# First MLP layer: the second product of the last two token blocks by seven block products, sums of weights on VectorE, a fourth raw buffer

## The chip, the cores and the metric
One core of a Trainium2 chip runs the whole program. TensorE (PE) multiplies, VectorE (DVE) and GpSimd (POOL) work element by element, ScalarE (ACT) does functions and copies, SyncE (SP) issues most transfers (DMA), POOL the accumulating ones. The metric is the device time of one execution, in microseconds (us); three runs of the kernel before are shown.

## The reference
Chunked attention over 3072 tokens, then two MLP layers in float32:

```
x = attention(q, k, v, mem_k, mem_v)        # 3072 x 512, windows of 32 queries
h = x @ w_in;   g = softplus(h)             # 512 -> 2048
y = g @ w_out                               # 2048 -> 512: the product that is changed
h2 = y @ w_in2; g2 = prelu(h2, alpha)       # second layer
out = g2 @ w_out2
```

## The kernel before
Tokens go in six blocks of 512 (`NB`). A float32 operand is a high and a low part, and a product takes three matmuls (high high, high low, low high). All matmuls of the MLPs have 128 x 128 weights against 512 columns.

**First layer.** There are 96 steps (`steps`), one for a block and 128 of the 2048 hidden features (`f`, 16 for each block). A step has `pe_h` (12 matmuls into `ps_hh`, one of two banks), softplus on ACT (`act_first`, tile `ta`), the high part on ACT (`high`, tile `g`), the low part on DVE (`low`), and `pe_out` (12 matmuls that add to four banks `ps_o`, one for each quarter of the 512 outputs). The two banks for `ps_hh` mean that step i+2 can't start before the softplus of step i has read its bank. `drain_one` and `drain_to` bring a finished block to `y_dram`. Attention of later blocks (24 tiles of 128 tokens: scores `s`, maximum `m`, shift `c`, `exp` on ACT, sum `n`, share `w`, transposes `t`, copy `pt`, values `v*`, split into `x`) lies between the steps. Softplus and exp need different tables on ACT, so an exp stands between two loads of a table.

**Weights.** `load_raw` brings float64 words into a pool of three rooms (`raw`), DVE turns them into float32 (`ab` to `cv`), ACT and DVE or POOL split them (`high_w`, `low_w`). Weights of the second layer are brought in during the first; `weight_sums` makes four sums of each set of blocks on POOL (tile `wsum`), `split_task` splits blocks and sums, and all go to DRAM (`in_ops`, `out_ops`).

**Second layer.** Blocks go in pairs. `quad` makes the first product and `second` the second product, each by seven block products in place of eight (`PASSES`: S1, A11, S4, S2, S3, A12, A22), 8 items for each pass, 6 matmuls for each item, into `ps_q`. In `second`, `load_w_out` brings 1 MB for every four items, POOL's accumulating DMAs (`SUMS`) and `prepare` (loads and sums of `y` for the next pair, tiles `yraw`, `yt`, `xop`) lie beside it. The last step's `pe_out` runs within the first `quad` (`between`).

**Order.** Up to about 90 us it is written by hand (`OPENING`). Behind that `schedule` gives every piece an engine, a length, a due time (with offsets in `O`), what it comes after, and rooms that it takes and gives; `Plan.run` lists them, and engines then take their instructions in that order, each in its own queue. SP and POOL queues too are in order: an issue that waits holds all behind it.

Of the kernel before, what the change touches and what calls it, by code (L numbers as in the profile page):

```python
# [57 lines left out]
HK = 2 * P  # L58

# [28 lines left out]
RUNS = 8  # L88
O = {'km': -55.97, 's': 11.7, 'm': 28.21, 'c': 66.61, 'e': 31.62, 'n': 45.26, 'r': -92.5, 'w': 94.58, 't': 85.64, 'pt': 82.79, 'v': -20.27, 'xh': 136.06, 'xl': -8.55, 'first': 47.53, 'gap': -183.71, 'second': 20.97, 'gap2': -27.69, 'raw': 41.75, 'ab': -85.86, 'cl': -61.09, 'ca': 10.82, 'cb': 74.39, 'cc': -95.76, 'wh': -29.12, 'wl': -22.45, 'odd': 97.94, 'sp': 116.5, 'hi': 37.44, 'lo': 2.59, 'out': 17.61, 'wait': 0.05, 'sloads': -125.79, 'km0': 68.55, 'km1': 28.97, 's0': -25.87, 's1': 2.3, 'm0': -192.19, 'm1': -112.61, 'c0': -31.95, 'c1': -25.21, 'e0': -51.53, 'e1': -16.47, 'n0': -131.79, 'n1': 72.42, 'r0': -17.47, 'r1': -5.18, 'w0': 52.91, 'w1': -43.08, 't0': -1.99, 't1': 39.24, 'pt0': -100.96, 'pt1': 70.29, 'v0': 21.52, 'v1': 14.34, 'xh0': -72.64, 'xh1': 5.24, 'xl0': 133.53, 'xl1': -30.69, 'by0': -46.78, 'by1': 30.48, 'va': -0.63, 'vb': 176.94, 'vc': -46.03, 'vd': 155.73, 'ra': -58.02, 'rb': 154.89, 'rc': 130.18, 'wld': 105.54, 'dra': -108.27, 'ca0': 58.14, 'ca1': -5.43}
# [33 lines left out]
class Plan:  # L123
# [16 lines left out]
    PORT = {"ab", "ab2", "cl", "cl2", "ca", "cb", "cv", "cv2", "n", "r", "w", "lo", "wl", "km", "sums2", "sl2", "wd", "ysum", "yd", "y4"}  # L140
# [87 lines left out]
def attention_mlp_mlp_kernel(ctx: ExitStack, tc, qk, v, w1, w2, consts, out):  # L228
# [11 lines left out]
    rpool = ctx.enter_context(room_pool("raw", 3))  # L240
# [12 lines left out]
    y_dram = dpool.tile([DM, NTOK], F32, name="y_dram")  # L253
    in_ops = dpool.tile([NQ, P, 2, 7, HK], F32, name="in_ops")
# [55 lines left out]
    def high_w(k):  # L310
        if k % 2 == 0:
            W[k // 2] = wpool.tile([P, 2, 2 * DM], F32R, tag="w", name="wsplit")
        act.copy(out=W[k // 2][:, 0, k % 2 * DM:(k % 2 + 1) * DM], in_=words[0, k])

    def low_w(k, eng):
        w = W[k // 2][:, :, k % 2 * DM:(k % 2 + 1) * DM]
        eng.tensor_tensor(out=w[:, 1, :], in0=words.pop((0, k)), in1=w[:, 0, :].bitcast(F32), op=ALU.subtract)
# [20 lines left out]
    def weight_sums(q, second):  # L338
# [291 lines left out]
    def drain(ps_of, b):  # L630
        for m, ps in enumerate(ps_of):
            if m % 2 == 0:
                room = rpool.tile([P, 2, DM], F32, tag="raw", name="o_sb")
            drain_one(m, ps, room[:, m % 2, :])
            drain_to(m, room[:, m % 2, :], b, False)

# [16 lines left out]
    def pe_out(i):  # L653
        b, f, first, final = steps[i]
        if first:
            acc[b] = acc_banks()
        out_sums(acc[b], g_sp.pop(i), W[f][:, :, DM:], first, final)
        if final and i == len(steps) - 1:
            drain(acc.pop(b), b)
# [5 lines left out]


# [7 lines left out]
    def raw_y(name):  # L674
        return late["x"].tile([P, N2], F32, tag="yraw", name=name, bufs=6)
# [8 lines left out]
    def sum_y(p, h, n):  # L684
        if n == 0:
            y_raw[p, h, T2] = raw_y("yt")
            y_raw[p, h, T3] = raw_y("yt")
# [278 lines left out]
    def prepare(p):  # L966
# [4 lines left out]
        for h in range(2):  # L971
            load, add, last, split = ((1, 8, 12, (11, 13, 15, 17, 19, 21, 23)), (19, 26, 30, (29, 31, 38, 44, 45, 47, 48)))[h]
# [26 lines left out]
    def schedule(when):  # L999

        plan = Plan({"h": 2, "ta": 2, "g": 1, "pa": 2, "s": 1, "tb": 1, "tb2": 1, "pair": 1, "tb0": 1, "tb1": 1, "word": 3, "raw": 3, "qk": 1, "v": 1,
                     "acc": 4, "y": 6, "w": NF, "x": 2})
# [10 lines left out]
        for n, k in enumerate(order):  # L1013
# [8 lines left out]
            add(("wh", k), "ACT", 0.62, need - O["wh"], lambda k=k: high_w(k), [("cv", n)] + ([("ds", 15)] if k == 26 else []) + ([("wh", k - 1)] if k % 2 else []), [] if k % 2 else ["w"])  # L1022
# [4 lines left out]
        for i, (b, f, first, final) in enumerate(steps):  # L1027
            t = when[i]
            x = [("xl", TB * b + c) for c in range(TB)]
            add(("h", i), "PE", 2.72, t, lambda i=i: pe_h(i), [("wl", 2 * f)] + (x if f == 0 else []) + ([("h", i - 1)] if i else []), ["h"])  # L1030
# [3 lines left out]
            if i == last:  # L1034
                break
            add(("out", i), "PE", 2.72, t + O["out"], lambda i=i: pe_out(i), [("lo", i), ("wl", 2 * f + 1)] + ([("out", i - 1)] if i else []),
                ["acc"] * 4 if first else [], ["g"] + (["w"] if i > last - NF else []))
            if final:
                room = ["w"] if f < HALF else ["x"]
                def begin(i=i, f=f):  # L1040
                    staged[i] = ((wpool if f < HALF else xpool).tile([P, 4, DM], F32, tag="w" if f < HALF else "x", name="o_sb"))
                add(("db", i), "", 0.0, t + 12, begin, [("out", i)], room if f < HALF else [])
# [6 lines left out]
                add(("ds", i), "", 0.0, 0, nothing, [("dd", i, m) for m in range(4)], [], room if f < HALF else [])  # L1049
# [7 lines left out]
        def tile(t, prev, due, step=None):  # L1057
# [22 lines left out]
            after_s += ([("t", TB - 1)] if t == TB else []) + ([("pt", prev)] if t > 2 * TB else []) + ([("h", step)] if step else [])  # L1080
            after_s += [("xl", TB + c) for c in range(TB)] if t == 2 * TB else []
            joint = t > 3 * TB
# [11 lines left out]
            else:  # L1094
                add(("c", t), "DVE", 0.6, due - when_due("c"), lambda: a_shift(t), [("m", t)], [], [] if start or joint else [sb])
# [35 lines left out]
        for j in range(4 * NQ):  # L1131
            q, e = divmod(j, 4)
            k, due = halves[j], when[24 + 64 * j // (4 * NQ)]
            dma(("raw2", j), 0.4, 1.9, due - 8, lambda j=j: load_raw(1, halves[j]), [("cv2", j - 1)] if j else [("raw", 2 * NF - 1)], ["raw"])
# [4 lines left out]
            def split_task(name, src, n, to, after, us, give):  # L1139
# [9 lines left out]
                add(("sl2",) + name, "POOL", us, due + 5, low_piece, [("sh2",) + name], [], give)  # L1149
                dma(("ss2",) + name, 0.45 * len(to), n / DM * 1.9, due + 6, store_piece, [("sl2",) + name], [], ["raw"])  # L1150

            if e % 2:
                z, k0 = e // 2, 4 * q + e // 2
                add(("sums2", q, z), "POOL", 3.2, due + 3, lambda q=q, z=z: weight_sums(q, z),
                    [("cv2", j)] + ([("sl2", q - (not z), 1 - z, 4)] if j > 1 else []), ["raw"])
# [3 lines left out]
                split_task((q, z, 0), lambda k=wide: words[1, k], DM, operands_at(q, z, A12 if z else A11, 2), [("sums2", q, z)], 1.4, ["word"])  # L1159
                split_task((q, z, 1), lambda k=narrow, part=part: words[1, k][:, part], HK, operands_at(q, z, A11 if z else A22, 1), [("sl2", q, z, 0)], 0.9, ["word"])  # L1160
                for n in (0, 2):
                    split_task((q, z, 2 + n), lambda q=q, z=z, n=n: sums[q, z][:, n:n + 2, :], DM, operands_at(q, z, S1 + n, 2),
                               [("sl2", q, z, 1 + n)], 1.4, ["raw"] if n else [])
                    if n == 0:
                        add(("sl2", q, z, 3), "", 0, 0, lambda: None, [("sl2", q, z, 2)])

        add("switch", "", 0, 0, switch_pools, [("xl", t) for t in range(NT)])
        for h in range(2):
            due = when[last - 8 + 4 * h]
            dma(("yl", h), 1.6, 3.2, due, lambda h=h: load_y(0, h), ["switch"], ["y"] * 4)  # L1170
            add(("ysum", h), "DVE", 2.1, due + 8, lambda h=h: [sum_y(0, h, n) for n in range(3)], [("yl", h)], ["y"] * 2)
# [96 lines left out]
```

## Time and profile before
| | us |
|---|---|
| runs shown (median) | 1085.9, 1088.45, 1087.64 (1087.64) |
| the profiled execution, its own time | 1090.2 |
| span of its instructions | 1088.1 |
| PE busy | 1066.2 (98%) |
| DVE, ACT, POOL busy | 704.4, 543.1, 171.8 |

The span is counted from the first to the last instruction; 2.1 us of the execution lie around it. "Busy" of an engine is the time in which one of its instructions was under way. The profile names the helper's line for all instructions, so tiles tell them apart: `ps_hh` and `ps_o` are the first layer's products, `ps_q` the second layer's, `ps_a` attention.

### The profile page before, as it was taken

How to read it: one execution, taken by the hardware profiler on the slowest of the kernel's cores; microseconds unless marked ns; L12 is line 12 of the kernel's file. 1: busy time of each engine (PE TensorE's matmuls, PEld its weight loads, DVE VectorE, ACT ScalarE, POOL GpSimd, SP SyncE). 2: the span in 40 equal slices, each digit the busy share in tenths (PEclk: the TensorE clock that was granted, in tenths of full speed). 3: DMA queues.
4: the chain of work that ended last, by engine and by line, in shares of the span. 5: the costliest groups of instructions: out<-in, count | busy, mean ns of one | idle time of the engine just before them, and what ended most of it. 6: DMA issues, size and time to landing. Idle time of an engine off the chain costs nothing.

```text
span 1088.1 us, 18751 instructions
## 1 busy us (share of the span) xinstructions
PE 1066.2 (98%) x7281; PEld 871.0 (80%) x7281; DVE 704.4 (65%) x1182; ACT 543.1 (50%) x940; POOL 171.8 (16%) x213
## 2 busy tenths in 40 slices
PE   6799999999999999999999999999999999999998
PEld 4568888778888888888888888888888888888886
DVE  5789988655554564345455156678666779566976
ACT  4564435455453454444344255664555755456643
POOL 0010112434234233222323100000000010000000
PEclk9989999999999999999999999999999999999999
DMA  8885674767656564535355173799875999856904
GB/s 203 209 188 182 188 196 126 187 184 192 197 165 183 175 170 128 187 120 166 111 180 191 61 288 126 282 282 322 200 280 174 327 298 256 259 203 256 372 0 78
DMA packets 156441, 214.69 MB, mean 197 GB/s; under 512 B 78656, under 2 KB 108480, under 8 KB 149440
## 3 DMA queue, kind: packets, MB, share of 16 engines
q1 hardware_dynamic: 152048, 196.58, 56.9%
q0 software_dynamic: 4032, 16.78, 8.1%
q8 instruction: 57, 0.93, 0.4%
q14 instruction: 32, 0.26, 0.1%
q10 hardware_dynamic: 272, 0.13, 0.0%
HBM read 154.74 MB, written 46.14 MB: 185 GB/s over the span
## 4 chain that ended last, share of the span: by engine, by line
PE 92%; DMA 5%; SPq 2%; DVE 1%; issue 0%; DVEq 0%
PE ps_q L76 42%; PE ps_hh L76 23%; PE ps_o L76 23%; PE ps_a L76 3%; DMA raw<-in_w_dram 3%; SPq L76 2%; DMA v<-in_v_dram 1%; DVE word L76 1%; DMA qk<-in_qk_dram 0%; DVE x L76 0%; DVE g L76 0%; DVE sm L76 0%; DVE wsplit L76 0%; DVE v L76 0%; DVE c L76 0%
## 5 line engine op out<-in xcount | busy, mean ns | idle before, releaser
L76 PE MATMUL ps_hh<-x,wsplit 128*128 128x512 f32 x1152 | 282.5, 394 | 1.9 <-DVE x L76 1.1
L76 PE MATMUL ps_o<-g,wsplit 128*128 128x512 f32 x1152 | 280.4, 392 | 0.8 <-DVE g L76 0.8
L76 PEld LDWEIGHTS ps_hh<-x,wsplit 128*128 128x128 f32 x1152 | 216.7, 189 | 49.0 <-DVE x L76 1.6
L76 PEld LDWEIGHTS ps_o<-g,wsplit 128*128 128x128 f32 x1152 | 214.3, 188 | 46.0 <-DVE g L76 1.1
L76 PE MATMUL ps_q<-xop,win 128*128 128x512 f32 x1008 | 229.1, 389 | 0.0
L76 PE MATMUL ps_q<-g,wout 128*128 128x512 f32 x1008 | 229.1, 389 | 0.0
L76 PEld LDWEIGHTS ps_q<-g,wout 128*128 128x128 f32 x1008 | 189.0, 188 | 39.5
L76 PEld LDWEIGHTS ps_q<-xop,win 128*128 128x128 f32 x1008 | 189.2, 188 | 39.3
L76 DVE TENSOR_TENSOR g<-ta,g 128x512 fp32r<-128x512 f32 x96 | 70.9, 738 | 132.5 <-ACT g L76 132.2
L76 ACT CAST g<-gb 128x512 fp32r<-128x512 f32 x168 | 100.8, 622 | 89.8 <-PE ps_q L76 66.1
L76 DVE TENSOR_TENSOR g<-gb,g 128x512 fp32r<-128x512 f32 x168 | 114.2, 686 | 35.2 <-ACT g L76 33.2
L76 ACT CAST g<-ta 128x512 fp32r<-128x512 f32 x96 | 59.6, 621 | 120.8 <-PE ps_o L76 120.6
L76 ACT ACTIVATE ta<-ps_hh 128x512 f32<-128x512 f32 x96 | 57.5, 599 | 119.8 <-PE ps_hh L76 116.5
L76 DVE SCALAR_TENSOR_TENSOR word<-raw,word 128x512 int32<-128x512 int32 x128 | 91.5, 715 | 2.7
L76 ACT ACTIVATE tp<-gb 128x512 f32<-128x512 f32 x48 | 30.4, 633 | 91.4 <-DVE gb L76 91.4
L76 POOL TENSOR_TENSOR wst<-wsum,wst 128x512 fp32r<-128x512 f32 x32 | 45.0, 1406 | 127.0 <-ACT wst L76 121.3
L76 DVE SCALAR_TENSOR_TENSOR gb<-gb,tp 128x512 f32<-128x512 f32 x48 | 33.2, 692 | 44.0 <-ACT tp L76 44.0
L76 DVE TENSOR_SCALAR word<-word 128x512 f32<-128x512 f32 (+1 forms) x128 | 57.3, 452 | 2.1
L76 POOL TENSOR_TENSOR wst<-word,wst 128x512 fp32r<-128x512 f32 (+1 forms) x32 | 34.2, 1068 | 140.3 <-ACT wst L76 135.1
L76 DVE TENSOR_SCALAR word<-raw 128x512 int32<-128x512 int32 x64 | 30.0, 471 | 39.8 <-DMA raw<-in_w_dram 26.9
L76 ACT ACT_TABLE_LOAD x38 | 48.8, 1283 | 11.1 <-DVE nm L76 10.5
L76 POOL DMA_DIRECT2D gb<-gb x12 | 10.4, 864 | 277.3 <-DVE g L76 168.4
(87 smaller groups left out, 860.6 us busy)
## 6 DMA issues: line engine op xcount, KB each, us to landing
wout<-out_ops SPq DMA_DIRECT2D x42, 1024.0 KB
raw<-in_w_dram SPq DMA_DIRECT2D x64, 512.0 KB
win<-in_ops SPq DMA_DIRECT2D x24, 1024.0 KB
win<-in_ops SPq DMA_DIRECT2D x24, 768.0 KB
out_ops<-wst SPq DMA_DIRECT2D x56, 256.0 KB
in_ops<-wst SPq DMA_DIRECT2D x24, 512.0 KB
gb<-gb POOLq DMA_DIRECT2D x12, 1024.0 KB, 13.7
qk<-in_qk_dram SPq DMA_DIRECT2D x24, 320.0 KB
```

What stands on the lines that cost most here:

```text
L76: i = getattr(self.engine, name)(*args, **kw)
```

## The change
For blocks 4 and 5 (`LP` = 4) steps have `pe_h` and softplus only. `g_first` and `g_kept` keep the results in eight 1 MB tiles (`gb`), the even features negated or with their differences. Behind them stand 56 items of six matmuls (`last_out`) into banks named `ps_q`, by the same seven passes as in `second`, with `g_high` on ACT and `g_low` on DVE ahead of each; four DMAs and eight additions on POOL make their sums (`BYDMA`, `("gs", ...)`). Their weights come from a new DRAM tile `outs_1`: the plain blocks stored as they are split (`("ac", ...)`), the sums made anew from the two parts on DVE (`whole_again`, `sums_of_first`, `low_part`), split, stored, and loaded by `load_last`. The loads of `y` for the second layer's first pair, `prepare`'s work of that pair and the first `win` lie beside these items.

W is laid out by two steps and by product (`weight`), so that rooms of w_out come free while w_in is used. The second layer's sums move from POOL to DVE for the first 8 of 16 sets (`BYPOOL`), and their low and high parts are made 1024 wide at once. `raw` has 4 rooms in place of 3, `yraw` 4 in place of 6; the tile `s` of late attention is now `pt`. The offsets `O` are other numbers, and a plan is chosen by the end of all pieces (`whole`).

```diff
-    rpool = ctx.enter_context(room_pool("raw", 3))
+    rpool = ctx.enter_context(room_pool("raw", 4))
...
+    def whole_again(q):
+        t = sums[q] = parts_room(q == 0)
+        w = W[q, 1].bitcast(F32)
+        dve.tensor_tensor(out=t[0].bitcast(F32).rearrange("p a k -> p (a k)"), in0=w[:, 0, :], in1=w[:, 1, :], op=ALU.add)
+
+    def sums_of_first(q):
+        t = sums[q]
+        a11, a21, a12, a22 = (t[0].bitcast(F32)[:, k, :] for k in range(4))
+        four_sums(dve, t[1], a11, a12, a21, a22)
...
+    def g_kept(i):
+        b, f, _, _ = steps[i]
+        a = g_a.pop(i)
+        if b == LP:
+            dve.tensor_scalar(out=slot(f % 2 * 2, f // 2), in0=a, scalar1=-1.0, scalar2=None, op0=ALU.mult)
+        else:
+            dve.scalar_tensor_tensor(out=slot(1, f // 2), in0=G[0, f // 2], scalar=-1.0, in1=a, op0=ALU.mult, op1=ALU.subtract)
...
+    def last_out(n):
+        i, q = divmod(n, NQ)
+        ka = PASSES[i][0]
+        more = ka == A12
+        if q == 0:
+            last_ps[ka] = last_ps[A11] if more else [bank({A11: "h", S4: "pa"}.get(ka, "acc")) for _ in range(2)]
+        g, w = g2.pop(n), w_out[-1, n // 4][:, n % 4]
+        for m in range(2):
+            for k, (a, e) in enumerate(((0, 0), (0, 1), (1, 0))):
+                pe.matmul(
+                    last_ps[ka][m], lhsT=w[:, a, m * P:(m + 1) * P], rhs=g[:, e, :], start=not more and q == 0 and k == 0,
+                    stop=q == NQ - 1 and k == 2, skip_group_check=more,
+                )
...
+            add(("gh", n), "ACT", 0.62, due - O["gh"], lambda n=n: g_high(n), after + ([("gh", n - 1)] if n else []), g)
+            add(("gl", n), "DVE", 0.72, due - O["gl"], lambda n=n: g_low(n), [("gh", n)])
...
-    pairs(lambda: pe_out(last))
+    pairs(lambda: None)
```

PE's order around block 4's steps. Before, `ps_hh` (first product) and `ps_o` (second) alternate, attention (`ps_a`) between them:

```order
L76 MATMUL ps_hh<-x,wsplit 128x512 x12
L76 MATMUL ps_a<-cst,s_sb 128x128 x4
L76 MATMUL ps_o<-g,wsplit 128x512 x12
L76 MATMUL ps_hh<-x,wsplit 128x512 x12
L76 MATMUL ps_a<-pt,v 64x32 x32
L76 MATMUL ps_a<-qk 32x64 x32
L76 MATMUL ps_o<-g,wsplit 128x512 x12
```

Now, from the middle of block 4 to the second layer (`ps_q<-g,wout` ahead of the first `ps_q<-xop,win` are the new items):

```order
L80 MATMUL ps_hh<-x,wsplit 128x512 x48
L80 MATMUL ps_a<-cst,pt 128x128 x4
L80 MATMUL ps_hh<-x,wsplit 128x512 x12
L80 MATMUL ps_a<-pt,v 64x32 x32
L80 MATMUL ps_hh<-x,wsplit 128x512 x180
L80 MATMUL ps_q<-g,wout 128x512 x6
L80 MATMUL ps_hh<-x,wsplit 128x512 x12
L80 MATMUL ps_q<-g,wout 128x512 x6
L80 MATMUL ps_hh<-x,wsplit 128x512 x12
L80 MATMUL ps_q<-g,wout 128x512 x6
L80 MATMUL ps_hh<-x,wsplit 128x512 x12
L80 MATMUL ps_q<-g,wout 128x512 x318
```

The second products of blocks 4 and 5 have left the places between the first products and stand behind them, 318 of their 336 matmuls in one stretch. ACT's order at an exp within block 4's steps, before (`ta` is softplus, `s_sb` the exp, `g` and `wst` high parts):

```order
L76 ACTIVATE ta<-ps_hh 128x512
L76 CAST wst<-word 128x256
L76 ACT_TABLE_LOAD
L76 ACTIVATE s_sb<-s_sb 128x512
L76 CAST g<-ta 128x512
L76 ACT_TABLE_LOAD
L76 ACTIVATE ta<-ps_hh 128x512
```

And now, with the queue's waits:

```order
L80 ACTIVATE ta<-ps_hh 128x512 [waits PE_49,Activation_49]
L80 ACT_TABLE_LOAD
L80 ACTIVATE pt<-pt 128x512 [waits DVE_49]
L80 ACT_TABLE_LOAD [waits PE_49]
L80 ACTIVATE ta<-ps_hh 128x512 [waits Activation_49]
L80 CAST wst<-wst 128x1024 [waits DMAHW2_49,DMAHW1_49,Pool_49]
L80 ACTIVATE ta<-ps_hh 128x512 [waits DVE_49,PE_49,Activation_49]
```

The cast of `g` is gone, a 1024 wide cast that waits for POOL and transfers stands ahead of a softplus. DVE's order late in the new items (`yt<-yraw` is the first sum of the second half of `y`):

```order
L80 TENSOR_TENSOR g<-gb,g 128x512 x2
L80 TENSOR_TENSOR yt<-yraw 128x512
L80 TENSOR_TENSOR yt<-yraw,yt 128x512
L80 TENSOR_TENSOR yraw<-yraw 128x512
L80 TENSOR_TENSOR g<-gb,g 128x512 x3
```

The sums stand ahead of the low parts of items 45 to 47 here. Before, sums of `y` for the first pair stood among first-layer steps, like this:

```order
L76 TENSOR_TENSOR g<-ta,g 128x512
L76 TENSOR_TENSOR yt<-yraw 128x512
L76 TENSOR_TENSOR yt<-yraw,yt 128x512
L76 TENSOR_TENSOR yraw<-yraw 128x512
L76 TENSOR_TENSOR g<-ta,g 128x512
```

What moved is the cover: there a low part was wanted every two products, here for every item of six matmuls.

## Rows read from the trace of the kernel before

**Rows 1.** Page, part 1: busy us (share of span) and instructions.
```profile
PE 1066.2 (98%) x7281; PEld 871.0 (80%) x7281; DVE 704.4 (65%) x1182; ACT 543.1 (50%) x940; POOL 171.8 (16%) x213
```

**Rows 2.** PE's waits, whole span: us in total, times, longest.
```profile
PE ps_s L76 <- POOL qk L76: 6.8, 5, 2.7
PE ps_x L76 <- DMA v<-in_v_dram: 2.3, 3, 1.6
...
PE ps_hh L76 <- DVE x L76: 1.1, 1, 1.1
```

**Rows 3.** Stretches: length, busy (instructions) of PE, PEld, DVE, ACT, POOL; PEclk, DMA, GB/s.
```profile
40.00:60.00 20.00, 16.00 (x255) 12.12 (x256) 15.42 (x35) 11.53 (x18) 3.99 (x9) 0.91 0.89 197
...
520.00:540.00 20.00, 20.00 (x90) 16.57 (x89) 6.19 (x11) 6.18 (x11) 7.18 (x7) 1.00 0.30 102
...
700.00:720.00 20.00, 20.00 (x90) 16.48 (x89) 15.65 (x25) 13.83 (x25) 2.62 (x3) 1.00 1.04 336
720.00:740.00 20.00, 20.00 (x90) 16.56 (x89) 12.72 (x20) 12.00 (x22) 1.72 (x2) 1.00 1.02 293
740.00:760.00 20.00, 20.00 (x90) 16.54 (x89) 19.41 (x33) 10.40 (x18) 0.86 (x1) 1.00 1.03 320
760.00:780.00 20.00, 20.00 (x90) 16.57 (x89) 15.29 (x24) 10.27 (x18) 0.00 (x0) 1.00 0.83 185
```

**Rows 4.** Chain that ended last, in order of time: start, us, what.
```profile
614.80 2.72 PE ps_hh L76 x12
617.52 5.44 PE ps_o L76 x24
...
631.12 451.62 PE ps_q L76 x1992
```

**Rows 5.** SP's waits, 44 to 47 us.
```profile
SPq L76 <- DVE g L76: 1.6, 1, 1.6
```

**Rows 6.** Order of time, PE, 40 to 80 us: start, us, instruction, [idle before].
```profile
53.02 1.58 PE L76 MATMUL ps_s<-qk 64*32 64x64 f32 x64 [2.71 <-POOL qk L76]
...
77.15 7.12 PE L76 MATMUL ps_hh<-x,wsplit 128*128 128x512 f32 x23 [1.10 <-DVE x L76]
```

**Rows 7.** Order of time, ACT at an exp, 492 to 498 us.
```profile
494.06 1.28 ACT L76 ACT_TABLE_LOAD   x1
495.36 0.63 ACT L76 ACTIVATE s_sb<-s_sb 128x512 f32<-128x512 f32 x1
496.00 1.28 ACT L76 ACT_TABLE_LOAD   x1
497.30 0.60 ACT L76 ACTIVATE ta<-ps_hh 128x512 f32<-128x512 f32 x1
```

**Rows 8.** ACT's waits for rooms that a store holds, whole span.
```profile
ACT wst L76 <- DMA out_ops<-wst: 10.8, 12, 2.6
```

**Rows 9.** Costliest groups: count, busy us, mean ns, idle before.
```profile
L76 DVE TENSOR_TENSOR g<-gb,g 128x512 fp32r<-128x512 f32 x168 | 114.2, 686 | 35.2 <-ACT g L76 33.2
L76 ACT CAST g<-gb 128x512 fp32r<-128x512 f32 x168 | 100.8, 622 | 89.8 <-PE ps_q L76 66.1
```

**Rows 10.** SP's issue and DVE's use of the second half of `y`.
```profile
721.58 7.12 SPq L76 DMA_DIRECT2D yraw<-y_dram  x4
...
739.54 0.69 DVE L76 TENSOR_TENSOR yt<-yraw 128x512 f32<-128x512 f32 x1 [1.66 <-DMA yraw<-y_dram]
```

**Rows 11.** DMA issues: count, KB each, us to landing.
```profile
wout<-out_ops SPq DMA_DIRECT2D x42, 1024.0 KB
...
win<-in_ops SPq DMA_DIRECT2D x24, 1024.0 KB
win<-in_ops SPq DMA_DIRECT2D x24, 768.0 KB
...
gb<-gb POOLq DMA_DIRECT2D x12, 1024.0 KB, 13.7
```

More of the change, by code (lines that the diff above doesn't have):

```diff
@@ L656, in pe_out, with slot, g_first @@
             acc[b] = acc_banks()
-        out_sums(acc[b], g_sp.pop(i), W[f][:, :, DM:], first, final)
-        if final and i == len(steps) - 1:
-            drain(acc.pop(b), b)
+        out_sums(acc[b], g_sp.pop(i), weight(f, 1), first, final)
+    def slot(k, q):
+        if q % 4 == 0:
+            slots[k, q // 4] = wpool.tile([P, 4, N2], F32, tag="w", name="gb")
+        G[k, q] = slots[k, q // 4][:, q % 4, :]
+        return G[k, q]
+    def g_first(i):
+        b, f, _, _ = steps[i]
+        to = slot(3, f // 2) if b > LP and f % 2 else tpool.tile([P, N2], F32, tag="ta", name="ta", bufs=2)
+        act.activation(out=to, in_=h_ps.pop(i), func=AF.Softplus)
+        g_a[i] = to
@@ new lines, in load_last, with keep, came_of @@
+    def load_last(j):
+        t = w_out[-1, j] = wpool.tile([P, NQ // 2, 2, HK], F32R, tag="w", name="wout")
+        sp.dma_start(out=t.bitcast(F32), in_=outs_1[PASSES[j // 2][0], j % 2])
+    def keep(key, m, tag):
+        kept_1[key, m] = tpool.tile([P, N2], F32, tag=tag, name="u2", bufs={"tb": 1, "tl": 1, "word": 3}.get(tag, 2))
+        return kept_1[key, m]
+    def came_of(d, b, m):
+        if m == 0:
+            c_1[d, b] = rpool.tile([P, 2, N2], F32, tag="raw", name="c")
+        return c_1[d, b][:, m, :]
@@ L685, in sum_y @@
         if n == 0:
-            y_raw[p, h, T2] = raw_y("yt")
-            y_raw[p, h, T3] = raw_y("yt")
+            two = rpool.tile([P, 2, N2], F32, tag="raw", name="yt")
+            y_raw[p, h, T2], y_raw[p, h, T3] = (two[:, e] for e in range(2))
         to, a, b = ((T3, T1, B11), (T2, B22, T3), (T1, B22, T1))[n]
@@ L1048, in schedule @@
                         [("dr", i, m)], eng="POOL" if adds else "SP")
-                add(("ds", i), "", 0.0, 0, nothing, [("dd", i, m) for m in range(4)], [], room if f < HALF else [])
+                add(("ds", i), "", 0.0, 0, nothing, [("dd", i, m) for m in range(4)], [], room if over else [])
         add("corners", "DVE", 2.4, 0, no_corners)
@@ L1167, in schedule @@
-        add("switch", "", 0, 0, switch_pools, [("xl", t) for t in range(NT)])
+                split_task((q, z, 0), lambda k=wide: words[1, k], DM, operands_at(q, z, A12 if z else A11, 2), [("cv2", j if z else j - 1)], 1.4, ["word"])
+                split_task((q, z, 1), lambda k=narrow, part=part: words[1, k][:, part], HK, operands_at(q, z, A11 if z else A22, 1), [("cv2", j - 1 if z else j)], 0.9, ["word"])
+                for k in range(2):
+                    add(("wd2", q, z, k), "", 0, 0, nothing, [("sums2", q, z), ("sl2", q, z, k)], [], ["word"])
@@ new lines, in schedule @@
+        for q in range(NQ):
+            due = when[44 + 2 * q] - O["so"]
+            rooms = ["w"] if q else ["raw"] * 2
+            add(("rc", q), "DVE", 1.4, due - O["sq"], lambda q=q: whole_again(q), [("wl", 4 * q + 1), ("wl", 4 * q + 3), ("raw", 2 * NF - 1)] + ([("sl1", q - 1)] if q else []), rooms)
+            add(("sums1", q), "DVE", 1.65, due - O["sr"], lambda q=q: sums_of_first(q), [("rc", q)])
+            add(("sh1", q), "ACT", 1.05, due + 1, lambda q=q: high_part(sums[q]), [("sums1", q)])
+            add(("sl1", q), "DVE", 1.4, due + 1 - O["sc"], lambda q=q: low_part(dve, sums[q]), [("sh1", q)])
+            dma(("ss1", q), 0.9, 3.8, due + 2, lambda q=q: store_parts(sums.pop(q), sums_at(outs_1, q, 1)), [("sl1", q)], [], rooms)
+            dma(("ac", q, 0), 0.9, 1.9, when[24 + 3 * q] - O["ac"], lambda q=q: store_to(DM, W[q, 1][:, :, DM:], first_at(q, A12, 2)), [("wl", 4 * q + 1), ("wl", 4 * q + 3), ("raw", 2 * NF - 1)] + ([("i", "ac", q - 1, 1)] if q else []))
+            dma(("ac", q, 1), 0.45, 0.95, when[24 + 3 * q] - O["ac"], lambda q=q: store_to(HK, W[q, 1][:, :, :HK], first_at(q, A11, 1)), [("i", "ac", q, 0)])
+            add(("wf", q), "", 0, 0, nothing, [("out", LH - NF + 2 * q + 1), ("rc", q), ("ac", q, 0), ("ac", q, 1)], [], ["w"])
@@ L1168, in schedule @@
+        for k, n, m in ((3, 23, [("gs", 1, 3, q) for q in range(NQ)]), (0, 39, []), (2, 47, [("gs", 1, 2, q) for q in range(NQ)]), (1, 55, [])):
+            add(("sf", k), "", 0, 0, nothing, [("gl", n)] + m, [], ["w"] * 2)
         for h in range(2):
-            due = when[last - 8 + 4 * h]
-            dma(("yl", h), 1.6, 3.2, due, lambda h=h: load_y(0, h), ["switch"], ["y"] * 4)
-            add(("ysum", h), "DVE", 2.1, due + 8, lambda h=h: [sum_y(0, h, n) for n in range(3)], [("yl", h)], ["y"] * 2)
+            due = end + 10 + 26 * h
+            dma(("yl", h), 1.6, 2.9, due, lambda h=h: load_y(0, h), ["switch", ("out", last + 7)], ["y"] * 4)
+            add(("ysum", h), "DVE", 2.1, due + 8, lambda h=h: [sum_y(0, h, n) for n in range(3)], [("yl", h)], ["raw"])
@@ L1191, in attention_mlp_mlp_kernel, with whole @@
         when = came + [came[-1] + 2.72 * 2]
-    plan = min(plans, key=lambda x: x.done["out", last - 1])
+    def whole(x):
+        d = x.done
+        return max(d["out", last + 7 * NQ], d["win0",], d["win1",] - 8, d["yd", 1, T4] - 6, d["cc", 1, 0, 1] - 3, max(d.values()) - 6)
+    plan = min(plans, key=whole)
     for name, (since, until) in plan.idle.items():
```

214 lines of the change are left out of this document (155 added, 59 removed).

## The prediction
> **What bounds the kernel now.** The first view is the page's list of busy times: PE is under way in 1066.2 of 1088.1 us [rows 1], so 21.9 us are all that waits and ends leave to gain, and anything larger must come from fewer matmuls. The second is PE's waits over the whole span: its waits are for `qk` from POOL (6.8 us in five), for `v` from DMA (2.3) and once for `x` from DVE (1.1) [rows 2], all of them before 78 us in the order of time; the last two are in [rows 6]. The third is a table of stretches: from 520 us on every 20 us have 20.00 us of PE at a granted clock of 1.00 [rows 3]. The fourth is the chain that ended last, which gives the price of a matmul where PE never stops: 12 of the first product take 2.72 us, 24 of the second 5.44, and 1992 of the second layer 451.62 [rows 4], each time 0.2267 us. So behind the opening the time is the number of 128 x 512 matmuls times 0.2267 us, and every other engine counts only where it can't keep up with that.
>
> **Removed.** Blocks 4 and 5 have 2 x 16 steps of 12 matmuls in the second product, 384. Now there are 56 items of 6, 336. The first products, attention and the second layer keep their counts. 48 x 0.2267 = **10.9 us less**, all on PE's path.
>
> **The opening.** The order of PE, ACT and POOL up to about 80 us stays as it is. What changes is the fourth room of `raw`: SP's queue stands 1.6 us for a room that DVE has to free [rows 5], and behind that load in the same queue are loads of `qk` and `v`. These end, through POOL's copy of `qk`, at PE's idle 2.71 us ahead of `ps_s` at 53.02 and later at its 1.10 us for `x` at 77.15 [rows 6]. Best case: both go, −3.8. Worst: nothing goes, since DMA engines are at 0.89 of their time in 40 to 60 us [rows 3] and an earlier load only pushes others; a fourth load in flight might even delay a `qk` by up to 1 us, +1. I take SP's own wait, **−1.6**, the only part of it that the room removes by itself.
>
> **The steps without a second product.** Before, 5.44 us lay between two first products' starts; now, from step 64, they follow each other at 2.72 us on two banks, save for attention's matmuls. PE can go from step i+1 to i+2 without a stop if softplus i ends within 2.72 us of step i's end. Softplus is 0.60 us [rows 7], which leaves 2.12. An exp with its two table loads is 1.28 + 0.63 + 1.28 = 3.19 us [rows 7]. If it starts right behind softplus i−1, that is 0.60 us into a step of 2.72, softplus i starts 1.07 late and ends 1.67 after its step, and nothing stops. If it starts just when the step ends, softplus ends at 3.79, 1.07 over. The order leaves four tiles of attention that can meet this: 0 to 4.3 us. ACT's casts of `wst` that wait for stores are the other part: 12 waits of 10.8 us together, 0.9 on average, the longest 2.6 [rows 8]. The mean fits into 2.12, the longest passes it by 0.5; three such would make 1.5. So 0 to +6; I take one late exp, **+1.0**, since the exps hang on `m` and `c` from DVE, at 6.19 of 20 us in such a stretch [rows 3] and so rarely late.
>
> The Trainium skill speaks against this part: "ScalarE: Activation LUTs", section "What ACT_TABLE_LOAD costs", adds a drain of about 1380 ns to the load's 1283 ns, some 2.66 us for a switch. The trace bears out the load and not the drain: the softplus begins 1.30 us after the load began [rows 7]. By the page every switch back would take 2.66 + 0.60 = 3.26 us (an estimate from that page), 0.54 over the step, some 2 us in four tiles, and the forecast below would be 1079.5 in place of 1077.4.
>
> **The 56 items.** An item is 6 x 0.2267 = 1.36 us on PE; ahead of it are a cast on ACT of 0.622 and a subtraction on DVE of 0.686 us [rows 9]. Items 4 to 7 have two rooms `g` only, so a cast waits for the end of the item two before it: 1.31 us of work in 1.36, with hand-overs between. That is 0 to 0.2 us for each of about five items, up to +1; **+0.3**. Later items take rooms of `raw` too and run like the second layer's, on the same cast and subtraction, where PE doesn't stop.
>
> The second half of `y` needs rooms that DVE frees in the first half's sums. In the new order SP's last `yraw` load can be issued only about six items, 8.2 us, ahead of the low part of item 45, and DVE's sums stand ahead of that low part: a late load holds items up. Before, 10.8 us lay between the end of SP's issue (721.58 + 7.12 = 728.70) and the first sum at 739.54, and DVE waited 1.66 of it for the load [rows 10], while DMA engines were full (1.02 and 1.03) [rows 3]. By that row the load is up to 2.6 us late; with rooms in hand, items 42 to 44 hide one to two of these. 0 to +3; **+1.0**.
>
> **Costed at nothing.** DVE gets eight sets of w_out: a sum 1024 wide, four sums 256 wide and a low part 1024 wide. At 0.686 us for 512 columns [rows 9] that is about 1.4 + 1.4 + 1.4 = 4.2 us a set, 34 us; eight sets of sums from POOL are 1.4 each, 11 us. It uses 6.19 of 20 us in the stretch where they stand [rows 3], so in 200 us there would be some 138 free for these 45. Should that cover be gone, the low parts of steps are late; in 740 to 760 us, though, DVE was at 19.41 of 20 and PE still had its 20 [rows 3]. Stores to `outs_1` go out in the same stretch at DMA share 0.30 [rows 3]. The first item's weights are issued some four steps, 11 us, ahead of it, like the 1 MB of an accumulating DMA that lands in 13.7 us with its additions [rows 11]; if they are late, 1 to 3 us come on top, which I leave in the range.
>
> **The sum.** −10.9 − 1.6 + 1.0 + 0.3 + 1.0 = −10.2. The profiled execution took 1090.2 us, so 1080.0 in its like. The median of the shown runs, 1087.64, is 2.6 lower: **1077.4 us**.
>
> **Rivals.**
> *ACT sets the pace in steps 64 to 95.* All four exps fall late, or casts that wait stand ahead of softplus: +4.3 to +6 in place of +1.0, so 1080.7 to 1082.4 us. For it: in the new order a 1024-wide cast with waits for POOL and two transfers stands directly ahead of a softplus. Against it: ACT has about 0.60 of 2.72 us taken by softplus in these steps, as the cast of `g` has gone. Chance 0.15.
>
> *DMA sets the pace in the items: slower than before.* Their weights are 14 x 1.05 MB = 14.7 MB, the four accumulating DMAs 4.2, `y` 2.1 in and 2.1 out, and two pairs of `win` 2 x (1.05 + 0.79) = 3.7 (sizes: [rows 11]); 26.8 MB in the items' 76 us and some 20 us ahead of them, 280 GB/s. In 700 to 780 us the chip moved 336, 293, 320 and 185 GB/s, 283 on average, with DMA engines full in the first three [rows 3]. So it fits, with little over. At 280 nothing is lost. At 248 GB/s the transfers need 108 us, 12 more: the gain is used up. At 240 they need 111.7 us, and the time is 1077.4 + 15.7 = 1093 us. For it: accumulating transfers read as much as they write. Against it: 320 and 336 were held beside like work, and the demand for weights alone is 1.05 MB in 5.44 us, as in the second layer before. It decides from about 245 GB/s down. Chance 0.07.
>
> *The change doesn't deliver.* If all 56 items were bound by their rooms at 0.1 to 0.2 us each, 5.6 to 11.2 us would go back: 1083 to 1088.6. Against it: only eight items are confined to two rooms. Chance 0.05, mostly within 0.2%.
>
> *The opening gives both waits.* −3.8 in place of −1.6: 1075.2, and 1073 to 1074 if the items and the exps cost nothing too. Chance 0.11.
>
> **How the numbers follow.** Forecast 0.62, ACT 0.15, DMA 0.07, no delivery 0.05, opening 0.11. The range is from 1072.9, all costs at nothing and both opening waits gone (1090.2 − 10.9 − 3.8 − 2.6), to 1083, ACT's upper end: **1073 to 1083**, which leaves out the last two unfavourable cases. A measurement of this kernel tells about 0.2%, 2.2 us, from no change. Faster by more: 0.62 + 0.15 + 0.11 + 0.01 = 0.89; within it 0.04; slower 0.07.
>
> **What would show it.** In the profile after: 336 more matmuls into `ps_q` and 384 fewer into `ps_o`; 0.2267 us a matmul on the chain from the last first product to the end. PE's waits should have the opening's entries, smaller than 2.71 and 1.10, and the start of the uninterrupted PE some 1.6 us ahead of 77.15. A wait of `ps_hh` for `ta` over 4 us in total means ACT's rival; a wait of `ps_q` for `wout` by DMA, with DMA share at 1 over the whole of the items, means the DMA rival; many short waits of `ps_q` for `g` on DVE mean rooms; one wait for `g` behind `yt` means the late `yraw`. The forecast is wrong if PE's idle behind 80 us is over 8 us, or if the opening is longer than before: then the load order, and not the matmul count, decides.

## The result: slower, since a load of y in the second layer comes late

| | before | after |
|---|---|---|
| median of the runs, us | 1086.88 (4 runs) | 1095.64 (4 runs: 1093.45, 1095.38, 1095.89, 1096.64) |
| the profiled execution, its own time | 1090.2 | 1093.45 |
| span of its instructions | 1088.1 | 1091.7 |

The ratio to before is 1.0076 (interval 1.0056 to 1.0097): 0.8% slower, where the prediction had 1077.4 us and 0.89 on faster. The profiled execution is the fastest of the four, 2.2 us below their median.

The page's first part and PE's waits over the whole span (us in total, times, longest) answer to [rows 1, 2]:

```profile
PE 1058.8 (97%) x7229; PEld 861.2 (79%) x7233; DVE 793.2 (73%) x1318; ACT 561.3 (51%) x958; POOL 161.8 (15%) x177
```

```profile
PE ps_q L80 <- DVE g L80: 8.7, 5, 6.5
PE ps_s L80 <- POOL qk L80: 4.9, 2, 2.7
PE ps_a L80 <- issue: 2.1, 1, 2.1
PE ps_o L80 <- issue: 1.6, 1, 1.6
PE ps_hh L80 <- DVE x L80: 1.5, 2, 1.1
```

PE is 7.4 us less busy (48 matmuls fewer at 0.2267 us would be 10.9; part of the difference is the clock, below), and yet the span is 3.6 us longer. The first line of the waits is new: `ps_q` is the second layer and the new items, where PE never waited before. PE's order of time (start, us, instruction, [idle before]) has the places and the borders of the stages:

```profile
73.84 5.55 PE L80 MATMUL ps_hh<-x,wsplit 128*128 128x512 f32 x23 [1.11 <-DVE x L80]
...
616.20 4.01 PE L80 MATMUL ps_q<-xop,win 128*128 128x512 f32 x17
...
692.36 2.90 PE L80 MATMUL ps_q<-g,wout 128*128 128x512 f32 x12
...
745.91 19.33 PE L80 MATMUL ps_q<-g,wout 128*128 128x512 f32 x74 [6.54 <-DVE g L80]
...
778.00 2.20 PE L80 MATMUL ps_q<-xop,win 128*128 128x512 f32 x9
...
854.15 2.21 PE L80 MATMUL ps_q<-g,wout 128*128 128x512 f32 x9
...
902.17 5.26 PE L80 MATMUL ps_q<-g,wout 128*128 128x512 f32 x18 [1.38 <-DVE g L80]
...
933.71 2.65 PE L80 MATMUL ps_q<-xop,win 128*128 128x512 f32 x11
```

The first layer with its new items ends at 616.20 us; before, it ended at 622.80 with 12 matmuls (2.72 us) still to come, so it has become 9.3 us shorter. Then the loss: the second product of the first pair (`ps_q<-g,wout`) takes 778.00 − 692.36 = 85.64 us where 336 matmuls at 0.2267 us make 76.17, and that of the second pair 79.56. Before they took 76.20 and 76.16. That is +12.8 us, and −9.3 + 12.8 = +3.5 us is, but for 0.1, the difference of the spans.

Stretches of the first of these two places, and, last, one of the second (length, busy of PE, PEld, DVE, ACT, POOL, then the granted clock, DMA share, GB/s), answer to [rows 3]:

```profile
739.00:744.00 5.00, 0.37 (x2) 0.00 (x0) 0.00 (x0) 1.14 (x2) 0.00 (x0) 0.99 1.01 277
744.00:751.00 7.00, 5.09 (x13) 3.99 (x14) 6.44 (x11) 0.04 (x1) 0.00 (x0) 0.52 1.01 376
751.00:760.00 9.00, 9.00 (x41) 7.45 (x40) 9.00 (x16) 5.15 (x9) 0.00 (x0) 1.00 0.25 67
...
902.00:910.00 8.00, 7.39 (x29) 5.16 (x30) 8.00 (x15) 2.81 (x5) 0.00 (x0) 1.00 1.00 298
```

PE and DVE stand still together, DMA engines are full. The wait costs more than its 6.54 us: over 744 to 751 us the granted clock is 0.52 (0.50, the lower of its two levels, in 746 to 750), and 13 matmuls fill 5.09 us in place of 2.95. At the second place the wait is 1.38 us and the clock stays at 1.00, yet the stage loses 3.4 us: DVE is busy for all of the 8 us behind the wait, and PE gets through at most 29 matmuls where 35 would fit. So what is late on DVE is made up only slowly. What they wait for stands in DVE's order of time and in the chain that ended last:

```profile
736.36 0.69 DVE L80 TENSOR_TENSOR yt<-yraw 128x512 f32<-128x512 f32 x1 [1.63 <-DMA yraw<-y_dram]
...
744.56 0.69 DVE L80 TENSOR_TENSOR yt<-yraw,yt 128x512 f32<-128x512 f32 x1 [6.91 <-DMA yraw<-y_dram]
745.17 0.68 DVE L80 TENSOR_TENSOR g<-gb,g 128x512 fp32r<-128x512 f32 x1
```

```profile
725.08 19.39 DMA yraw<-y_dram
```

A sum of `y` for the next pair waits for its fourth load; the low part `g` stands behind it in DVE's queue, and PE waits for that. The load is 256 KB and takes 19.39 us from issue to landing.

### The profile page after: what moved, and what is told of

It reads as the page before. It is cut to its first block, busy times and chain, and to the rows that moved or that the text cites. A ratio compares the mean times of both kernels' runs of the same rounds, so it can differ in the third digit from the quotient of the medians.

```text
span 1091.7 us, 18778 instructions
## 1 busy us (share of the span) xinstructions
PE 1058.8 (97%) x7229; PEld 861.2 (79%) x7233; DVE 793.2 (73%) x1318; ACT 561.3 (51%) x958; POOL 161.8 (15%) x177
## 4 chain that ended last, share of the span: by engine, by line
PE 86%; DMA 6%; DVE 5%; ACT 1%; issue 1%; SPq 0%; POOL 0%; DVEq 0%; ACTq 0%
PE ps_q L80 45%; PE ps_hh L80 22%; PE ps_o L80 15%; PE ps_a L80 3%; DMA yraw<-y_dram 3%; DMA raw<-in_w_dram 2%; DVE word L80 1%; DVE g L80 1%; ACT v L80 1%; DVE sm L80 1%; DVE x L80 0%; DVE pt L80 0%; DMA qk<-in_qk_dram 0%; ACT g L80 0%; DVE nm L80 0%
## 5 line engine op out<-in xcount | busy, mean ns | idle before, releaser
L80 PE MATMUL ps_q<-g,wout 128*128 128x512 f32 x1344 | 311.3, 392 | 9.2 <-DVE g L80 8.7
L80 PEld LDWEIGHTS ps_q<-g,wout 128*128 128x128 f32 x1344 | 252.8, 189 | 66.5 <-DVE g L80 14.0
L80 ACT CAST g<-gb 128x512 fp32r<-128x512 f32 x224 | 133.0, 621 | 129.2 <-PE ps_q L80 107.4
L80 DVE TENSOR_TENSOR g<-gb,g 128x512 fp32r<-128x512 f32 x224 | 154.0, 700 | 61.5 <-ACT g L80 59.6
L80 PE MATMUL ps_o<-g,wsplit 128*128 128x512 f32 x768 | 188.2, 393 | 2.9 <-issue 1.6
L80 PEld LDWEIGHTS ps_o<-g,wsplit 128*128 128x128 f32 x768 | 142.4, 188 | 33.7 <-DVE g L80 2.1
L80 DVE TENSOR_TENSOR g<-ta,g 128x512 fp32r<-128x512 f32 x64 | 53.5, 836 | 39.6 <-ACT g L80 39.5
L80 POOL TENSOR_TENSOR wst<-word,wst 128x512 fp32r<-128x512 f32 (+2 forms) x40 | 44.6, 1120 | 143.5 <-ACT wst L80 128.2
L80 POOL DMA_DIRECT2D gb<-gb x16 | 13.8, 862 | 331.4 <-DVE g L80 193.8
L80 ACT ACT_TABLE_LOAD x38 | 48.8, 1283 | 13.5 <-DVE nm L80 10.8
L80 ACT CAST g<-ta 128x512 fp32r<-128x512 f32 x64 | 39.8, 622 | 21.8 <-PE ps_o L80 21.0
L80 POOL TENSOR_TENSOR wst<-wst 128x1024 fp32r<-128x1024 f32 x16 | 42.0, 2623 | 20.7 <-ACT wst L80 18.6
## 6 DMA issues: line engine op xcount, KB each, us to landing
gb<-gb POOLq DMA_DIRECT2D x16, 1024.0 KB, 13.8
```

The source lines that it names most:

```text
L80: i = getattr(self.engine, name)(*args, **kw)
```

## Why the load is late: the experiments

Two things of the change meet here. `yraw` has four rooms in place of six (two sums went to `raw`), and since a room can only be asked for behind its last reader, `prepare` was re-timed for pairs two and three:

```diff
-            load, add, last, split = (..., (19, 26, 30, (29, 31, 38, 44, 45, 47, 48)))[h]
+            load, add, last, split = (..., (24, 30, 34, (33, 36, 38, 44, 45, 47, 48)))[h]
```

The second half's load is asked for at item 24, behind six 1 MB loads of w_out in SP's queue instead of five, its sums at 30. SP's order of time answers to [rows 10]; the last line is from the kernel before and stands there directly ahead of the load:

```profile
688.57 26.08 SPq L80 DMA_DIRECT2D wout<-out_ops  x6
714.75 10.65 SPq L80 DMA_DIRECT2D yraw<-y_dram  x4
...
698.15 9.52 SPq L76 DMA_DIRECT2D wout<-out_ops  x5
```

Counted from the stage's start, the last load is issued at 32.7 us (725.08 − 692.36). Before, SP's four loads end at 728.70, 27.0 us from the stage's start at 701.68. **Theory one** was the room: the fourth becomes free 6 us too late. **Its rival** was the place in the queue and the full DMA engines.

**The rooms sooner.** The first half's `T3` and `T4` are split ahead of `T1` and `T2`, so that the fourth room is free at 27 us:

```diff
-            for n, k in zip(split, (B11, B21, B22, T1, T2, T3, T4)):
+            for n, k in zip(split, (B11, B21, B22, T1, T2, T3, T4) if h else (B11, B21, B22, T3, T4, T1, T2)):
```

> The changed kernel, with one edit in the preparation of y beside the second products of the first two pairs: of the first half the operands T3 and T4 are split before T1 and T2, so that the fourth room for yraw comes free some 6 us sooner (27 instead of 33 us into the stage); loads, sums and accumulating transfers keep their places. Theory (the fourth load is issued too late because there are four rooms): it lands in time, both second products go from 85.6 and 79.6 us back to about 76.2 us, the time falls by 10 to 13 us to 1082 to 1085 us. Rival (its place in SP's queue and the full DMA engines make it late, not its room): the stages keep 82 us or more together with 78, the time stays above 1090 us.

Measured: 1092.08 us (10 runs, 1090.08 to 1098.74), ratio to before 1.0052 (1.0032 to 1.0073). The last load now is issued at 721.51 us, 26.7 us into the stage, and still takes 19 us. SP's order, and the chain that ended last:

```profile
690.72 26.41 SPq L80 DMA_DIRECT2D wout<-out_ops  x6
717.22 4.61 SPq L80 DMA_DIRECT2D yraw<-y_dram  x4
```

```profile
721.51 19.22 DMA yraw<-y_dram
```

In the profiled execution the two stages take 78.9 and 83.3 us. So the room alone isn't it; theory one falls as it stood.

**The place only.** As above, and the load stands at item 19 again, its sums stay at 30. Against the kernel of the experiment ahead, nothing moves but one 1 MB load of w_out in SP's queue in each of the two stages, from ahead of the four loads to behind them:

```diff
-... (24, 30, 34, (33, 36, 38, 44, 45, 47, 48))
+... (19, 30, 34, (33, 36, 38, 44, 45, 47, 48))
```

> As e1_rooms_sooner, with one more edit: the second half's load of y stands at item 19 (behind five loads of w_out in SP's queue in place of six), its sums and splits stay at items 30 to 48. Theory, mended (the 1 MB load of w_out ahead of it in the same queue, and not DVE's order, makes the load late): no wait for it, both second products 76.2 us, 1082 to 1085 us, as e6_rooms_and_places. Rival (the sums at items 30 to 32 stand at a worse place of DVE's order): stages of 78 us or more, over 1087 us.

Measured: 1083.06 us (10 runs, 1080.91 to 1086.3), ratio to before 0.9964 (0.9948 to 0.9979), 9.0 us under the experiment ahead. SP's order and all waits of PE behind 76 us:

```profile
688.03 9.88 SPq L80 DMA_DIRECT2D wout<-out_ops  x5
711.82 7.12 SPq L80 DMA_DIRECT2D yraw<-y_dram  x4
```

```profile
PE ps_o L80 <- issue: 1.8, 1, 1.8
PE ps_a L80 <- issue: 1.0, 1, 1.0
PE ps_q L80 <- DVE g L80: 0.8, 3, 0.3
PE ps_a L80 <- DVE pt L80: 0.6, 1, 0.6
```

The fourth load is issued 26.7 us into the stage as before the edit (718.6 − 691.93), both stages take 76.5 us, and no sum waits. So, with the room free at 27 us, one megabyte ahead in the queue decides. The room alone was not enough; whether the place alone would be is not shown, since an earlier place with the room free only at 33 us was not run.

**Rooms and places as before.**

```diff
-... (24, 30, 34, (33, 36, 38, 44, 45, 47, 48))
+... (19, 26, 30, (29, 31, 38, 44, 45, 47, 48))
```

> As e1_rooms_sooner, and the second half's load, sums and splits stand at the items where the kernel before has them (load at item 19, sums from 26, in place of 24 and 30). Theory: as in the kernel before, both second products take 76.2 us; 1081 to 1085 us. Rival (DMA or DVE is fuller for another reason in the changed kernel): still over 80 us for the first of them, over 1088 us.

Measured: 1083.43 us (5 runs), ratio 0.9961 (0.9948 to 0.9974), stages of 76.21 and 76.18 us. The same as with the sums at 30: with the load in time, DVE's sums can stand at either place.

**Only this in the kernel before.** Four rooms, the two sums in a room of their own, the items 24, 30 to 48:

```diff
-        return late["x"].tile([P, N2], F32, tag="yraw", name=name, bufs=6)
+        return late["x"].tile([P, N2], F32, tag="yraw", name=name, bufs=4)
...
-            y_raw[p, h, T2] = raw_y("yt")
-            y_raw[p, h, T3] = raw_y("yt")
+            two = late["x"].tile([P, 2, N2], F32, tag="yt", name="yt", bufs=1)
+            y_raw[p, h, T2], y_raw[p, h, T3] = (two[:, e] for e in range(2))
```

> The kernel before, with only this of the change: four rooms for yraw in place of six, the sums T2 and T3 in a room of their own, and the second half's load, sums and splits at items 24, 30 to 48 as in the changed kernel. Theory (these alone make the stall): the second products of the first two pairs take about 85 and 79 us in place of 76.2, the time rises by 8 to 15 us to 1095 to 1102 us. Rival (the stall needs something else of the change): within 3 us of 1087 us.

Measured: 1093.1 us (5 runs, up to 1104.01), ratio 1.0073 (1.0032 to 1.0115): +5.8 us over its own runs of the kernel before (1087.27), between what theory and rival had said. These parts alone do make a loss; why it is smaller is not shown. SP's order is that of the changed kernel:

```profile
697.54 25.95 SPq L76 DMA_DIRECT2D wout<-out_ops  x6
723.59 10.65 SPq L76 DMA_DIRECT2D yraw<-y_dram  x4
```

Its profiled execution, the fastest of the five, shows the smaller part of it, stages of 78.3 and 76.7 us.

**Without the sums that POOL's transfers make meanwhile.** The accumulating transfers at items 30 and 35 are left out in the first two pairs.

```diff
-            elif n in SUMS:
+            elif n in SUMS and n < 30:
```

> The changed kernel without the accumulating transfers at items 30 and 35 of the second products of the first two pairs (these sums are left out). Theory (the late load's last packets stand beside these transfers): the load lands within 10 us of its issue in place of 19, PE waits under 1 us at each place, the time falls to 1082 to 1086 us. Rival (the room or SP's queue alone makes it late): PE still waits 3 us or more in the first of the two stages.

Measured: one run, 1084.0 us, stages of 76.54 and 76.53 us, with loads issued as late as in the changed kernel (716.86 + 10.65 us). So the late place hurts only because of these transfers, as far as one run tells. What they do shows in two stretches of the changed kernel, between two accumulating transfers (728.4 to 732) and beside the next two (732.4 to 744.5). A line sorts the packets by size; then come packets, MB, share of the 16 engines' time, by queue; q1 is SP's, q0 POOL's:

```profile
DMA packets 562, 1.41 MB, mean 393 GB/s; under 512 B 73, under 2 KB 73, under 8 KB 495
q1 hardware_dynamic: 550, 1.39, 97.1%
q0 software_dynamic: 12, 0.02, 3.4%
```

```profile
DMA packets 488, 3.33 MB, mean 275 GB/s; under 512 B 43, under 2 KB 43, under 8 KB 94
q0 software_dynamic: 242, 1.84, 72.8%
q1 hardware_dynamic: 246, 1.50, 31.1%
```

Beside an accumulating transfer the two queues move nearly as many packets each, 246 and 242, but POOL's take 72.8% of the time and SP's queue is left 0.12 MB/us of the 0.39 that it moved alone. The Trainium skill, "DMA: Bandwidth & Descriptors", section "Queues, rings and completion order", has it that a DMA engine takes turns, packet by packet, between the queues for which it has work. The equal counts agree with that; no run shows the single turns.

The sizes show who is caught. The four loads of `y` are 512 packets of 2 KB (128 rows of 512 floats for each load), and no others in these stretches lie between 2 and 8 KB. In the gap of 3.6 us 495 − 73 = 422 of them pass; beside the next two transfers it takes 12 us for 94 − 43 = 51. In the kernel of "the place only" the gap is at 728 to 731.8 us, and from there to 745 none is left:

```profile
DMA packets 502, 3.78 MB, mean 286 GB/s; under 512 B 41, under 2 KB 41, under 8 KB 41
```

So a load of `y` that gets through before the gap ends is in time, and the last tenth of it, if it is still queued then, waits among the packets of the next transfers. That is how being some 6 us late (32.7 in place of 27.0 us into the stage) cost 13 us in two stages. That the spread of the times from run to run has the same cause is likely, but not shown: each kernel has one trace.

**Other parts of the change.** PE's remaining waits between 200 and 305 us of the changed kernel were suspected to come from what the change moved there. POOL's low parts of sums in halves, in the kernel of "rooms and places as before":

```diff
-        eng.tensor_tensor(out=t[1], in0=t[1].bitcast(F32), in1=t[0].bitcast(F32), op=ALU.subtract)
+        for a in (0, 2) if eng is pool else ():
+            eng.tensor_tensor(out=t[1][:, a:a + 2], in0=t[1][:, a:a + 2].bitcast(F32), in1=t[0][:, a:a + 2].bitcast(F32), op=ALU.subtract)
...
```

> e6_rooms_and_places, and POOL's low parts of the second layer's weight sums are made by two instructions 512 wide in place of one 1024 wide (2.62 us). Theory (an instruction of DVE that meets one of POOL stands still until it ends, so that PE's waits of some 5 us between 200 and 305 us come from the long instructions): these waits fall by 1 to 3 us, the time to 1080 to 1083 us. Rival (DVE waits for two short ones as long as for one, or these waits come from the transfers): within 1 us of 1083.4 us.

Measured: 1082.36 us (5 runs, 1079.35 to 1086.28), ratio 0.9954 (0.9928 to 0.9981); PE's waits there still are 2.2, 1.6 and 0.5 us. No difference from 1083.43 that could be told. With the edit to halves on the kernel of "the place only":

> e7_place_only with POOL's low parts in two halves as in e8_halves_on_pool: the changed kernel with the late load and nothing else mended. 1080.5 to 1083.5 us, that is 4 to 7 us under the kernel before; about 5 us of PE waits between 200 and 305 us and 1.3 us in the first items remain.

Measured: 1083.56 us (6 runs), ratio 0.9956 (0.994 to 0.9971), against 1083.06 without it: nothing again. PE's waits there are 1.9 and 1.8 us.

The eight sets of sums back on POOL in the kernel of "the place only", all other instructions in their order:

```diff
-... lambda q=q, z=z, eng=eng, raw=raw: weight_sums(q, z, eng, raw),
+... lambda q=q, z=z, raw=raw: weight_sums(q, z, pool, raw),
```

> e7_place_only with the eight sets of the second layer's weight sums that the change gave to DVE made on POOL again, every other instruction in its place. Theory (the move to DVE is worth something here only if POOL's longer way is late for somebody): PE's waits between 200 and 305 us stay within 2 us of those in e7, the time within 2 us of 1083 us. Rival (the sums on DVE delay low parts of g): these waits fall by 2 us or more, to 1080 to 1081 us.

Measured: 1085.42 us (10 runs, 1081.68 to 1089.46), ratio 0.9976 (0.9962 to 0.999); its interval overlaps with that of 1083.06 us. PE's waits there don't fall (the longest is 3.8 us in the profiled execution, the slowest of the ten). So nothing shows that they come from the sums on DVE.

The stores of plain blocks to `outs_1` later, behind every third first product, in the plan's order of the kernel of "the place only":

```diff
...
+    for x in plan.order:
+        if x[3] in later:
+            continue
+        moved.append(x)
+        if x[3][0] == "h" and x[3][1] >= 22 and (x[3][1] - 22) % 3 == 0 and (x[3][1] - 22) // 3 < NQ:
+            moved += [later[("i", "ac", (x[3][1] - 22) // 3, e)] for e in range(2)]
...
```

> e7_place_only with the 24 stores of plain blocks to outs_1 (in the changed kernel all between 148 and 178 us) moved in SP's queue behind every third first product from step 22 on; the order of the other engines stays. Theory (these 6.3 MB fill the DMA engines, so that stores of y and loads of raw words behind them are late and PE waits some 2 us near 204 us): this wait falls under 1 us, the time by 1 to 2 us, to 1081 to 1082 us. Rival (the wait near 204 us doesn't hang on them): the wait stays, within 1 us of 1083 us.

Measured: 1081.09 us (4 runs, 1079.51 to 1082.35), ratio 0.9937 (0.9921 to 0.9952): the lowest median of all, 6.8 us under the kernel before. The time is what the theory said, but not by its way: the wait near 204 us is still 1.8 us, and what stands ahead of it is the same, a low part of `x` on DVE that waits for a store:

```profile
205.47 0.69 DVE L80 TENSOR_TENSOR x<-ps_a,x 128x512 fp32r<-128x512 f32 x1 [3.20 <-DMA y_dram<-o_sb]
```

Its 2 us under the kernel that it is built on may be chance: the two were not measured side by side, and their intervals overlap.

Two experiments let the plan choose a new order for such a part and say nothing on the part itself. The first puts POOL's 1024-wide low parts on DVE (`"DVE", 1.4` and `low_part(dve, ...)` in place of `"POOL", 2.6` and `low_part(pool, ...)`):

> e6_rooms_and_places with these low parts (16 of 1024 columns) on DVE in place of POOL, some 1.4 us each. Theory (POOL's long instructions hold DVE): PE's waits between 200 and 305 us fall to 3 us or less, 1079 to 1083 us. Rival (DVE has no room left there, 15 to 18 of 20 us busy): low parts of g come late and the time rises to 1085 us or more.

Measured: 1111.93 us, ratio 1.0231 (1.0207 to 1.0255). The second sets `EARLY, BYPOOL = 8, 0`:

> e6_rooms_and_places with all sums of the second layer's weights on POOL, as in the kernel before (BYPOOL 0 in place of 8). Theory (the eight sets that moved to DVE cost nothing that shows): within 2 us of 1083.4 us. Rival (they delay low parts of g between 200 and 305 us): these waits of some 5 us fall to under 2, and the time to 1079 to 1081 us.

Measured: 1109.25 us, ratio 1.0198 (1.0174 to 1.0222). In both, PE waits at quite other places (18.3 us for attention's `pt` in the first, 6.7 us for a cast in the items in the second), perhaps since the offsets that fit one plan don't fit another. Only the runs that kept the order could be read.

## Why the prediction was wrong

**The term that failed** is that of `y`'s rooms. The prediction saw the mechanism (the last load can be issued only when DVE has freed rooms, the sums stand ahead of a low part, DMA engines are full) and priced it from [rows 10] at +1.0 us, up to 3. But it put it into the 56 items, and into these alone. [rows 10] are rows of the second layer, where the same four rooms serve the next two pairs, and where the change re-timed the load; that was put at nothing, without a reason. In the items the load was in time: behind 551.01 us they run to 616.20 without a stop. In the second layer it cost 9.4 and 3.4 us. The bound was wrong too: "up to 2.6 us late" was read from a load whose packets end inside the gap between two accumulating transfers; what misses the gap waits beside the next ones, and DVE's sum waited 6.91 us in place of 1.66. Two of the prediction's own signs came: a wait for `g` behind `yt`, and over 8 us of PE's idle behind 80 us (13.5).

**The matmuls**: right. 48 fewer at 0.2267 us; all terms together were given −10.2 us, and what they were meant for, the program up to the second layer, came to −9.3. That these are so near is in part luck, for the parts under that sum are less good.

**The opening**: a gain of 3.3 us in place of 1.6, but not shown to be the room's, and not in the way foretold. PE's uninterrupted work starts 3.3 us sooner, and in the other runs with four raw rooms whose opening is the same between 74.3 and 76.6 us (77.15 and 76.34 with three): one execution differs from the next by as much. Neither of the two waits that were to shrink has: 2.73 and 1.11 us now, 2.71 and 1.10 in [rows 6]. SP's wait of 1.6 us is there as before [rows 5]:

```profile
SPq L80 <- DVE g L80: 1.6, 1, 1.6
```

So the fourth room didn't remove that wait. In the other runs with the same opening it is 1.6, 0.3 or nothing. What shrank here is the sum of the waits for `qk` (4.9 us, 6.8 in [rows 2]) and for `v` (0.3, 2.3), but in the other runs with the same opening they are up to 7.3 and 2.5. A further 1.6 us is the granted clock: 23 matmuls take 5.55 us at 1.00 at the start of the stretch, 7.12 in [rows 6] at 0.76. That too is chance: with four rooms and the sums back on POOL they take 7.11.

**The steps without a second product**: ACT's rival was wrong, and so was the 1.0 us. PE's order of time runs through the whole stretch without idle:

```profile
473.58 11.33 PE L80 MATMUL ps_hh<-x,wsplit 128*128 128x512 f32 x48
...
489.11 41.10 PE L80 MATMUL ps_hh<-x,wsplit 128*128 128x512 f32 x180
```

180 matmuls take 41.1 us, 0.228 each. Three exps fall into block 4's steps, not four, and the first of them stands where second products still lie between. ACT's order has the last; ahead of it a softplus ends at 477.43, behind it the next starts 1.29 us after its table load began:

```profile
477.45 1.28 ACT L80 ACT_TABLE_LOAD   x1
478.74 0.63 ACT L80 ACTIVATE pt<-pt 128x512 f32<-128x512 f32 x1
479.55 1.28 ACT L80 ACT_TABLE_LOAD   x1 [0.17 <-PE ps_hh L80]
480.84 0.60 ACT L80 ACTIVATE ta<-ps_hh 128x512 f32<-128x512 f32 x1
```

The drain that the Trainium skill adds ("ScalarE: Activation LUTs", section "What ACT_TABLE_LOAD costs") shows neither ahead of a load nor behind it.

**The items**: the two rooms `g` cost three waits of 0.27, 0.26 and 0.26 us, 0.8 together (0.3 was taken, up to 1).

**Costed at nothing**: not quite. PE waits 2.1, 0.5, 1.6 and 0.6 us between 200 and 305 us, where the kernel before had one of 0.7; that is some 4 us more. The cover for them was read at a wrong place: in 520 to 540 us, the row with 6.19 us of DVE and a DMA share of 0.30, none of these sums and stores stands. The eight sets from POOL stand at 189 to 342 us, where DVE had up to 13.8 of 20 us before, and the 24 plain stores at 148 to 180, where the DMA share now is over 1. Still, with the sums back on POOL, or the stores later, these waits stayed. The first stands behind a low part of `x` that waits 3.42 us for a store of `o_sb` (1.66 before), in a stretch with a DMA share of 1.02; that this is its cause is argued. For the 1.6 us near 256 the trace names no releaser, and it stays open.

**The slower rival** named the right engines, the DMA engines, but as a rate over the items (from about 245 GB/s down). They moved 330 and 244 GB/s in 560 to 600 us and held nothing up. What came was one small load in a bad place, in the second layer.

## What to carry to other kernels

Who takes rooms from a pool must cost every later user of that pool, not only the stage for which the rooms were taken; here it was the second layer that paid for the first. A small load that many wait for belongs ahead of the large ones in its queue, above all where accumulating transfers share the DMA engines with that queue: once the room was free in time, one place in the queue decided 9 us. And a wait on PE can cost more than its length: here the clock behind it, or the engine that has to make up what was late.

## What was not expected of the hardware

- A 256 KB load took 19.39 us from issue to landing. Of its packets and those of the three loads ahead of it 422 of 512 went through in a gap between accumulating transfers, where SP's queue had 97.1% of the engines' time; the last 51 took 12 us beside the next two, where it had 31.1%.
- After a wait of 6.54 us PE had 0.52 of its clock for 7 us, which added about 2.1 us. Shorter waits differ: 2.1 us near 204 us left the clock at 1.00 in the changed kernel; in the experiment with rooms and places as before, a wait of the same place is followed by 0.57 for 4 us:

```profile
207.00:211.00 4.00, 4.00 (x40) 3.10 (x34) 3.45 (x8) 1.86 (x2) 0.00 (x0) 0.57 0.50 156
```

- A DVE instruction beside one of POOL took five times the mean of its kind. In the changed kernel:

```profile
195.24 4.19 DVE L80 TENSOR_TENSOR g<-ta,g 128x512 fp32r<-128x512 f32 x1 [1.31 <-ACT g L80]
```

```profile
195.10 3.77 POOL L80 TENSOR_TENSOR wst<-wst 128x1024 fp32r<-128x1024 f32 x1
```

The Trainium skill, "SBUF — State Buffer", section "Terms", has it that the port pair of these two engines is held for a whole instruction and the other one blocks; the row agrees, 4.19 us against a mean of 0.84 for this operation, and it ended 0.56 us after POOL's. PE had no wait beside it (20.00 us busy in 180 to 200).
